# Three low bits of the W1 and W2 words: taken on GpSimd by a product and a minimum, or on VectorE by a shift

## The chip, the core and the metric

One core of one Trainium2 chip runs the whole program. The metric is device time in microseconds (us) of one launch; less is better. The kernel before was timed in three runs, and one further execution was profiled.

## The reference

Three blocks follow each other, for a batch of 8 sequences of 576 rows:

```python
# attention over 32 pooled memory slots per head (8 heads of 64)
a = softmax(phi, axis=2); k_m = einsum('bhsm,bhsd->bhmd', a, k); v_m = einsum(..., a, v)
x = softmax(q @ k_m.T / 8) @ v_m                       # to (B, S, 512)
# first MLP
xn = (x - mean) / sqrt(var + 1e-6) * g_ln
x = x + relu(xn @ w_ch1) @ w_ch2                       # w_ch1 512x2048, w_ch2 2048x512
# second MLP with a spatial gate
h = gelu(x @ w_in); u, v = halves of h
gated = u * (w_sg @ layernorm(v) * g + b_sg)
out = x + gated @ w_out
```

The inputs are float32, except the weights `w_ch1`, `w_ch2` (W1 and W2 below), `w_in` and `w_out`: these are float64, and the kernel gets them as 64-bit words. To make a float32 of such a word the kernel needs the high 32-bit word, shifted and with its exponent moved, and the top three bits of the low 32-bit word.

## The kernel before, in words

The work is split in two phases. Phase 1 does attention and the first MLP, phase 2 the second MLP. In phase 1 a tile is 128 rows; each batch element is cut into two blocks of 256 to 320 columns. For each block `m1` (line 557) multiplies the attention weights with VW, the product of the pooled values and a 512-column quarter of W1; it has no own product x @ W1. ScalarE and VectorE make the ReLU of the result as a high and a low part (`hh` and `hl`, lines 543 and 544), and three steps later (LAG = 3) `m2` multiplies them with a 128-row chunk of W2 (lines 587 to 589). The ring of `hh` and `hl` has four buffers, that of `ph` two.

W1 comes in four quarters of four 128x512 pieces, W2 in sixteen 128x512 chunks: 32 pieces of 512 KB, each loaded once, from SyncE's queue, and converted once. All of this lies between 20 and 145 us of the span. For a piece of W1, `scale_w1` calls `to_f32` and ScalarE scales the result (`wc`, line 476); `center_w1` takes the column mean by TensorE (`cm`, line 482) and subtracts it on VectorE (line 484); `make_vw` multiplies with the pooled values (`pvw`, line 504) and writes `vw` (lines 514 and 515). For a chunk of W2, `split_w2` calls `split`, which makes the high part on ScalarE (line 124) and the low part on GpSimd (line 125). The same `split` with pieces of 256 columns converts `w_in` and `w_out`, in 24 calls around 600 to 850 us.

`to_f32` has three instructions: ScalarE's Prelu on the high word (line 110), VectorE's shift of the low word by 29 (line 111), and VectorE's instruction that shifts the high word and joins the two (line 112). It reads and writes every second 32-bit word of the raw tile, in place.

What sets the order: the program is traced by a list of events with times in steps (`at_time`), W1 quarters loaded at -26.5, -26.2, -2.5 and 2.0 and converted at -16.5, -5.0, 3.0 and 7.5, W2 chunk c loaded 5 units ahead of its conversion. A planner then sorts the instructions of each engine by readiness in a timeline that it works out itself; each engine runs its own list in order. `issue_after(ins)` adds an order edge behind `ins` only for instructions of the engine that `ins` is on. The gates given to `to_f32` are all VectorE instructions (the last `hl`, or, before the first block, an attention instruction on VectorE), so lines 111 and 112 stand behind the gate, and the Prelu on ScalarE does not.

Beside this, the attention of the first batch element runs at 25 to 62 us: scores (line 379), a transpose and a softmax on VectorE (lines 388 to 407) with the exponent on ScalarE (line 393), and the high and low parts of the attention weights, `aTh` and `aTl` (lines 418 and 419; the first `aTl` is on GpSimd). GpSimd's other work in the stretch is the low part of W2 (line 125), sums of exp(phi) (lines 276 to 281), the LayerNorm roots (lines 88 to 98) and `VBl` (line 329).

Of the kernel before, what the change touches and what calls it, by code (L numbers as in the profile page):

```python
# [15 lines left out]
ALU = mybir.AluOpType  # L16
# [12 lines left out]
def fused_kernel(ctx: ExitStack, tc: tile.TileContext, q, k, v, phi, g1, w1, w2, w_in, g2, w_sg, b_sg, w_out, out):  # L29
    nc = tc.nc  # L30
    PE, V, A, G = nc.tensor, nc.vector, nc.scalar, nc.gpsimd
# [11 lines left out]
    TB = 4  # L43
# [32 lines left out]
    wpool = ctx.enter_context(tc.tile_pool(name="wpool", bufs=19))  # L76

    def two(p, dtype, name):
        t = p.tile([P, 2, DM], dtype, tag="w", name=name)
        return t[:, 0, :], t[:, 1, :]  # L80
# [17 lines left out]
            G.tensor_tensor(out=y, in0=y, in1=t, op=ALU.mult)  # L98
        return y

    def to_f32(raw, gate=None):

        words = raw.bitcast(U32).rearrange("p (n two) -> p n two", two=2)
        lo, hi = words[:, :, 0], words[:, :, 1]

        gates = ExitStack()
        for ins in gate or ():
            gates.enter_context(tc.issue_after(ins.ins))
        with gates:
            A.activation(hi.bitcast(F32), hi.bitcast(F32), AF.Prelu, scale=2.0 ** -112, alpha=-(2.0 ** 32))  # L110
            V.tensor_scalar(lo, lo, 29, None, op0=ALU.logical_shift_right)
            V.scalar_tensor_tensor(out=lo, in0=hi, scalar=3, in1=lo, op0=ALU.logical_shift_left, op1=ALU.bitwise_or)
        return lo.bitcast(F32)

    def split(raws, wp, scale=None, gate=None):

        wh, wl = two(wp, F32R, "whl")
        n = DM // len(raws)
        for i, raw in enumerate(raws):
            cs = slice(i * n, (i + 1) * n)  # L120
            h, l = wh[:, cs], wl[:, cs]
            w = to_f32(raw, gate)
            if scale is None:
                A.copy(h, w)
                G.tensor_tensor(out=l, in0=w, in1=h.bitcast(F32), op=ALU.subtract)
            else:
                A.activation(h, w, AF.Copy, scale=scale)
                V.scalar_tensor_tensor(out=l, in0=w, scalar=scale, in1=h.bitcast(F32), op0=ALU.mult, op1=ALU.subtract)
        return wh, wl
# [11 lines left out]
    def phase1():  # L141
# [15 lines left out]
        st = {"lays": [], "ps0": 0}  # L157
# [297 lines left out]
        W2, WC, VW, raws = {}, {}, {}, {}  # L455

        def wc_tiles():
            return [tail.tile([P, 2, DM], F32, tag="wc", name="wc", bufs=4) for _ in range(2)]
# [11 lines left out]
        def scale_w1(fb):  # L470

            WC[fb] = ws = wc_tiles()
            for j, raw in enumerate(raws.pop(fb)):
                d = ws[j // 2][:, j % 2, :]
                w = to_f32(raw, [st.get("hl", tiles[TB - 1]["tr"])] if fb else None)
                A.activation(d, w, AF.Copy, scale=g1c[:, j:j + 1])

        def center_w1(fb):
# [43 lines left out]
        def split_w2(c):  # L522

            gate = st.get("hl", tiles[1 if c == 0 else 3]["tr"])
            W2[c] = split([raws.pop(("w2", c))], wpool, gate=[gate])


        hid, ybank, carry = {}, {}, {}
# [2 lines left out]
        for b in range(B):  # L531
            w = 18 * b
# [62 lines left out]
        tiles = [{"t": t} for t in range(NPAIR * TPP)]  # L595
# [15 lines left out]
        for b in range(B):  # L611
            pair, odd = divmod(b, 2)
            t0 = pair * TPP
            lo, hi = (t0 + 4, 4, 0, 2 * pair), (t0 + 4, 4, REM, 2 * pair + 1)
# [74 lines left out]
        for fb in range(NFB):  # L689
            at_time((-26.5, -26.2, -2.5, 2.0)[fb], load_w1, fb)  # L690
            at_time((-16.5, -5.0, 3.0, 7.5)[fb], scale_w1, fb)
            at_time((-16.4, -0.3, 4.6, 9.1)[fb], center_w1, fb)
            at_time((-15, 1.3, 5.8, 10.3)[fb], make_vw, 0, fb)
            at_time((1.4, 3.0, 7.4, 12.0)[fb], store_w1, fb)
        for c in range(NF):
            split_at = 4.5 * (c // 4) + 0.5625 * (c % 4) - 0.6 if c > 3 else 0.9 * c - 4
            at_time(split_at - 5 if c > 3 else -12.7 if c == 3 else 0.2 * c - 26.4, load_w2, c)
            at_time(split_at, split_w2, c)
# [20 lines left out]
        for n in range(len(steps) + LAG):  # L719
# [4 lines left out]
            if n >= LAG:  # L724
                _, j, c = steps[n - LAG]
# [31 lines left out]
    def convert_piece(p):  # L757
        kind, n = PIECES[p]
        w = split(R.pop(("piece", p)), wpool, 0.5 if kind == 2 else None, None if kind == 2 else R["relu"])
        if kind == 2:  # L760
            WO[n] = w
        else:
            WI[n, kind] = w
# [310 lines left out]
```

## Time and profile before

| what | value |
|---|---|
| median of three runs (lowest, highest) | 1216.44 us (1214.81, 1219.01) |
| the profiled execution's own time | 1217.86 us |
| its span | 1216.1 us |
| granted TensorE clock, mean | 0.987 |
| TensorE matmul busy | 1178.5 us, 97% of the span |
| VectorE / ScalarE / GpSimd busy | 692.4 / 465.8 / 400.6 us |

The span is the time from the first to the last instruction that the profile shows; 1.8 us of the execution's time lie around it. Busy shares are averages over stages that differ: the profile's rows by slices show where TensorE is not full, and the rows by instructions show what ended its waits.

### The profile page before, as it was taken

How to read it: one execution, taken by the hardware profiler on the slowest of the kernel's cores; microseconds unless marked ns; L12 is line 12 of the kernel's file. 1: busy time of each engine (PE TensorE's matmuls, PEld its weight loads, DVE VectorE, ACT ScalarE, POOL GpSimd, SP SyncE). 2: the span in 40 equal slices, each digit the busy share in tenths (PEclk: the TensorE clock that was granted, in tenths of full speed). 3: DMA queues.
4: the chain of work that ended last, by engine and by line, in shares of the span. 5: the costliest groups of instructions: out<-in, count | busy, mean ns of one | idle time of the engine just before them, and what ended most of it. 6: DMA issues, size and time to landing. Idle time of an engine off the chain costs nothing.

```text
span 1216.1 us, 20760 instructions
## 1 busy us (share of the span) xinstructions
PE 1178.5 (97%) x7711; PEld 986.2 (81%) x7711; DVE 692.4 (57%) x1669; ACT 465.8 (38%) x1064; POOL 400.6 (33%) x621
## 2 busy tenths in 40 slices
PE   4599999999999999999999999999999999999998
PEld 2277678878787878888778788889989988998997
DVE  3787665654754545744536546568576367447632
ACT  3575333222332223332223345445444354344430
POOL 2033212211110211211211212456566475656641
PEclk9599999999999999999999999999999999999999
DMA  8996544344413353513332234132250042023202
GB/s 201 270 293 180 164 109 121 95 118 103 105 57 107 82 143 91 131 53 93 84 96 69 81 102 128 35 81 71 78 148 27 19 131 86 1 73 94 78 18 70
DMA packets 199141, 124.15 MB, mean 102 GB/s; under 512 B 93312, under 2 KB 174336, under 8 KB 199040
## 3 DMA queue, kind: packets, MB, share of 16 engines
q1 hardware_dynamic: 199040, 122.82, 36.9%
q8 instruction: 61, 1.00, 0.3%
q14 instruction: 40, 0.33, 0.1%
HBM read 99.72 MB, written 31.33 MB: 108 GB/s over the span
## 4 chain that ended last, share of the span: by engine, by line
PE 88%; DVE 5%; DMA 4%; SPq 1%; issue 1%; ACT 1%; POOL 1%; DVEq 0%; POOLq 0%; ACTq 0%
PE ph L557 16%; PE py L587 11%; PE py L589 11%; PE py L588 10%; PE pvs L976 8%; PE po L999 8%; PE pv L867 8%; PE pu L951 7%; PE pvw L504 2%; PE kvp L299 2%; DMA raw<-in_moe_w_ch_dram 1%; SPq L83 1%; DMA q<-q_d 1%; PE cm L482 1%; PE px L435 1%
## 5 line engine op out<-in xcount | busy, mean ns | idle before, releaser
L557 PE MATMUL ph<-aTh,vw 128*128 128x320 f32 (+1 forms) x1024 | 244.6, 301 | 3.6 <-ACT vw L514 1.7
L587 PE MATMUL py<-whl,hh 128*128 128x512 f32 x512 | 204.5, 401 | 2.8 <-ACT hh L543 2.8
L588 PE MATMUL py<-whl,hh 128*128 128x512 f32 x512 | 202.0, 395 | 0.0
L557 PEld LDWEIGHTS ph<-aTh,vw 128*128 128x128 f32 x1024 | 177.6, 190 | 26.9 <-issue 9.1
L589 PE MATMUL py<-whl,hl 128*128 128x512 f32 x512 | 188.7, 398 | 0.0
L543 ACT ACTIVATE hh<-ph 128x256 fp32r<-128x256 f32 x256 | 97.2, 384 | 155.1 <-PE ph L557 88.0
L544 DVE SCALAR_TENSOR_TENSOR hl<-ph,hh 128x256 fp32r<-128x256 f32 x256 | 106.6, 420 | 83.4 <-ACT hh L543 82.1
L557 PE MATMUL ph<-aTl,vw 128*128 128x256 f32 (+1 forms) x512 | 152.6, 298 | 0.0
L587 PEld LDWEIGHTS py<-whl,hh 128*128 128x128 f32 x512 | 96.3, 188 | 32.9 <-issue 9.8
L976 PE MATMUL pvs<-wsh,vhl 128*128 128x288 f32 x576 | 120.9, 295 | 0.0
L588 PEld LDWEIGHTS py<-whl,hh 128*128 128x128 f32 x512 | 96.6, 189 | 20.8 <-issue 3.4
L951 PE MATMUL pu<-yTh,whl 128*128 128x288 f32 x512 | 110.9, 295 | 0.3 <-DVE ug L856 0.3
L557 PEld LDWEIGHTS ph<-aTl,vw 128*128 128x128 f32 x512 | 97.4, 190 | 10.0 <-issue 2.1
L589 PEld LDWEIGHTS py<-whl,hl 128*128 128x128 f32 x512 | 92.0, 189 | 15.4 <-issue 4.4
L976 PEld LDWEIGHTS pvs<-wsh,vhl 128*128 128x128 f32 x576 | 94.1, 188 | 0.6
L867 PE MATMUL pv<-whl,yTh 128*128 128x512 f32 x288 | 90.8, 395 | 0.0
L999 PE MATMUL po<-whl,gh 128*128 128x512 f32 x288 | 90.1, 391 | 0.0
L951 PEld LDWEIGHTS pu<-yTh,whl 128*128 128x128 f32 x512 | 85.1, 188 | 1.8 <-DVE ug L856 0.8
L543 ACT ACTIVATE cr<-ph 128x64 fp32r<-128x64 f32 x128 | 28.5, 222 | 127.2 <-PE ph L557 126.8
L976 PE MATMUL pvs<-wsl,vhl 128*128 128x288 f32 x256 | 75.4, 295 | 0.0
L951 PE MATMUL pu<-yTl,whl 128*128 128x288 f32 x256 | 75.4, 295 | 0.0
L979 POOL TENSOR_TENSOR gt<-gt,ug 128x288 f32<-128x288 f32 x64 | 52.9, 827 | 68.4 <-DVE gt L978 65.6
(153 smaller groups left out, 2165.4 us busy)
## 6 DMA issues: line engine op xcount, KB each, us to landing
wc<-w_d SPq DMA_DIRECT2D x28, 512.0 KB, 5.0
y_d<-x SPq DMA_DIRECT2D x36, 256.0 KB, 2.8
yt<-y_d SPq DMA_DIRECT2D x36, 256.0 KB, 2.7
yr<-y_d SPq DMA_DIRECT2D x36, 256.0 KB, 3.0
kv<-in_k_dram SPq DMA_DIRECT2D x32, 256.0 KB, 4.0
kv<-in_v_dram SPq DMA_DIRECT2D x32, 256.0 KB, 4.5
raw<-in_moe_w_ch_dram SPq DMA_DIRECT2D x32, 256.0 KB, 8.7
raw<-in_moe_w_ch_dram SPq DMA_DIRECT2D x16, 512.0 KB, 6.2
```

The lines of the kernel that those rows point to most:

```text
L299: mm = PE.matmul(kvp[32 * j:32 * j + 32], ph[:, 4 * g + j, c, :] if c < 4 else pr[rows, j, :], ts[c // 2][0][:, :, j, c % 2, :] if c < 4 e ...
L543: high = A.activation(out_h, src, AF.Relu)
L544: return high, V.scalar_tensor_tensor(out=out_l, in0=src, scalar=0.0, in1=out_h.bitcast(F32), op0=ALU.max, op1=ALU.subtract)
L557: PE.matmul(ph, w_[:, ks], x[:, g, 0:w], start=(n == 0), stop=(n == 3 * HK - 1))
L587: PE.matmul(py, hh, wh, start=start, stop=False)
L588: PE.matmul(py, hh, wl, start=False, stop=False)
L589: PE.matmul(py, hl, wh, start=False, stop=stop)
L867: PE.matmul(pv, y[:, kc, cs], w, start=(n == 0), stop=(n == 3 * KC - 1))
L951: PE.matmul(pu, w[:, ds_], y[:, kc, cs], start=(n == 0), stop=(n == 3 * KC - 1))
L976: PE.matmul(pvs, v_, w_, start=(n == 0), stop=(n == len(ops) - 1))
L979: G.tensor_tensor(out=gt, in0=gt, in1=ug, op=ALU.mult)
L999: PE.matmul(po, gg[:, dc, cs], w, start=(n == 0), stop=(n == 3 * KC - 1))
```

## The change

In the calls for W1 and W2 the low word goes to GpSimd, which multiplies it by 2^-29 and takes the minimum with 7, in one instruction that reads and writes 32-bit integers. The calls for `w_in` and `w_out` pass no engine and keep the shift on VectorE. The joining instruction of line 112 stays on VectorE.

```diff
-    def to_f32(raw, gate=None):
+    def to_f32(raw, gate=None, low=None):
...
-            V.tensor_scalar(lo, lo, 29, None, op0=ALU.logical_shift_right)
+            if low is None:
+                V.tensor_scalar(lo, lo, 29, None, op0=ALU.logical_shift_right)
+            else:
+                low.tensor_scalar(lo, lo, 2.0 ** -29, 7.0, op0=ALU.mult, op1=ALU.min)
...
-    def split(raws, wp, scale=None, gate=None):
+    def split(raws, wp, scale=None, gate=None, low=None):
...
-            w = to_f32(raw, gate)
+            w = to_f32(raw, gate, low)
...
-                w = to_f32(raw, [st.get("hl", tiles[TB - 1]["tr"])] if fb else None)
+                w = to_f32(raw, [st.get("hl", tiles[TB - 1]["tr"])] if fb else None, G)
...
-            W2[c] = split([raws.pop(("w2", c))], wpool, gate=[gate])
+            W2[c] = split([raws.pop(("w2", c))], wpool, gate=[gate], low=G)
```

## Rows read from the trace of the kernel before

**Rows 1.** The page: TensorE's busy tenths in 40 slices of the span.
```profile
PE   4599999999999999999999999999999999999998
```
**Rows 2.** Busy time by stretches: us, engines' busy us (instructions), clock, DMA share, GB/s.
```profile
25.00:45.00 20.00, 8.05 (x51) 3.28 (x49) 11.41 (x26) 10.03 (x17) 0.85 (x2) 0.72 1.04 249
45.00:57.00 12.00, 8.06 (x32) 4.19 (x32) 10.83 (x25) 5.93 (x12) 2.58 (x2) 0.50 1.04 262
57.00:65.00 8.00, 7.17 (x27) 5.01 (x28) 6.88 (x15) 5.52 (x11) 1.30 (x1) 0.73 1.03 385
65.00:145.00 80.00, 78.32 (x521) 59.53 (x519) 60.81 (x137) 44.92 (x101) 28.92 (x35) 1.00 0.74 207
```
**Rows 3.** Groups by shape, VectorE, the shift: busy us, mean ns, idle before.
```profile
L111 DVE TENSOR_SCALAR raw<-raw 128x512 uint32<-128x512 uint32 x32 | 14.6, 488 | 7.7 <-DMA raw<-in_moe_w_ch_dram 7.7
```
**Rows 4.** The same view for GpSimd: the nearest forms.
```profile
L125 POOL TENSOR_TENSOR whl<-raw,whl 128x512 fp32r<-128x512 f32 x16 | 20.8, 1314 | 54.1 <-ACT whl L124 49.1 <-issue 3.0 <-DMA raw<-in_moe_w_ch_dram 1.9
L402 POOL TENSOR_TENSOR z<-z,r 128x512 f32<-128x512 f32 x14 | 14.7, 1049 | 134.2 <-DVE r L401 59.0 <-ACT hh L543 28.6 <-ACT cr L543 14.2
L155 POOL MEMSET VBh<- 128x512 f32 x2 | 1.0, 524 | 0.0
```
**Rows 5.** ScalarE in order of time: start us, us, work, idle before.
```profile
33.45 0.67 ACT L110 ACTIVATE raw<-raw 128x512 f32<-128x512 f32 x1 [0.92 <-DMA raw<-in_moe_w_ch_dram]
...
40.32 0.67 ACT L110 ACTIVATE raw<-raw 128x512 f32<-128x512 f32 x1 [1.58 <-DMA raw<-in_moe_w_ch_dram]
40.89 0.61 ACT L393 ACTIVATE z<-z 128x512 f32<-128x512 f32 x1
42.56 0.66 ACT L110 ACTIVATE raw<-raw 128x512 f32<-128x512 f32 x1 [1.06 <-DMA raw<-in_moe_w_ch_dram]
...
49.96 0.66 ACT L110 ACTIVATE raw<-raw 128x512 f32<-128x512 f32 x1 [2.03 <-DMA raw<-in_moe_w_ch_dram]
```
**Rows 6.** VectorE in order of time.
```profile
37.67 0.69 DVE L391 TENSOR_REDUCE m<-z 128x16 f32<-128x512 f32 x1
41.53 0.69 DVE L399 TENSOR_REDUCE r<-z 128x16 f32<-128x512 f32 x1 [3.18 <-ACT z L393]
...
45.30 0.41 DVE L111 TENSOR_SCALAR raw<-raw 128x512 uint32<-128x512 uint32 x1
45.63 0.17 DVE L400 TENSOR_SCALAR r<-r 128x16 f32<-128x16 f32 x1
45.71 2.34 DVE L484 TENSOR_TENSOR wc<-wc,cm 128x1024 f32<-128x1024 f32 x2
...
53.74 2.44 DVE L111 TENSOR_SCALAR raw<-raw 128x512 uint32<-128x512 uint32 x7
```
**Rows 7.** TensorE in order of time.
```profile
36.02 6.04 PE L482 MATMUL cm<-wc,mean 128*128 128x512 f32 x8
46.98 3.06 PE L504 MATMUL pvw<-wc,kvT 64*32 64x512 f32 x16 [4.91 <-DVE wc L484]
...
57.83 2.08 PE L482 MATMUL cm<-wc,mean 128*128 128x512 f32 x2 [0.88 <-ACT wc L476]
```
**Rows 8.** TensorE's waits in the stretch of 105 to 115 us.
```profile
PE ph L557 <- DVE hl L544: 0.8, 1, 0.8
```
**Rows 9.** VectorE in order of time, late in phase 1's conversions.
```profile
110.02 1.55 DVE L111 TENSOR_SCALAR raw<-raw 128x512 uint32<-128x512 uint32 x1
...
141.20 1.27 DVE L400 TENSOR_SCALAR r<-r 128x4 f32<-128x4 f32 x1
```
**Rows 10.** GpSimd in order of time.
```profile
47.19 1.28 POOL L419 TENSOR_TENSOR aTl<-z,aTh 128x512 fp32r<-128x512 f32 x1 [21.27 <-ACT aTh L418]
...
109.98 1.30 POOL L125 TENSOR_TENSOR whl<-raw,whl 128x512 fp32r<-128x512 f32 x1
...
139.84 2.60 POOL L125 TENSOR_TENSOR whl<-raw,whl 128x512 fp32r<-128x512 f32 x2 [3.04 <-issue]
```
**Rows 11.** Durations of the joining instruction by tile: min, median, max ns.
```profile
L112 DVE SCALAR_TENSOR_TENSOR raw<-raw x32: 674/686/1236, 26.5 to 139.0; 128x512 uint32<-128x512 uint32 x32
```

## The prediction

> **What bounds the kernel now.** I read the slices of the page first: TensorE is at nine tenths or more from the third slice on, and only the first two (to 61 us) show 4 and 5 [rows 1]. So for 95% of the span any other engine's relief is worth nothing unless it ends a TensorE wait. The 32 conversions that the change touches all lie in 25 to 145 us, so I next took busy time by stretches there [rows 2]. In 25 to 45 us TensorE works 8.05 of 20 us, in 45 to 57 it works 8.06 of 12 at a granted clock of 0.50 (the 1.2 GHz level) with VectorE busy 10.83 of 12, and in 57 to 65 it works 7.17 of 8. In 65 to 145 it works 78.32 of 80. The time that VectorE could give back sits before 58 us, with 1.7 us of TensorE idle behind it.
>
> The views in order of time then say which wait ends last there. The weights land one piece per 2.2 us (starts at 40.32 and 42.56 that end a wait for a load [rows 5]), with the transfer engines fully busy [rows 2]. VectorE waits until 41.53 for the exponent of the softmax, and that exponent stood on ScalarE behind a Prelu that waited for a load until 40.32 [rows 5, 6]. From 41.53 to 45.71 VectorE works without a gap up to the centering of the first W1 quarter (line 484), for which TensorE sits idle 4.91 us until 46.98 [rows 6, 7]. The column means themselves were done at 36.02 + 6.04 = 42.06 [rows 7], so VectorE's chain is late there by 45.71 - 42.06 = 3.65 us. The second place is at 57.83: TensorE waits 0.88 us for `wc` of the second quarter, and in front of that on VectorE stand seven shifts of 2.44 us in all, and right behind them line 112 [rows 6, 7].
>
> **The change part by part.** Profiled execution: 1217.86 us, of which the span is 1216.1.
>
> *The removed shifts.* 32 x 488 ns, which is the 14.6 us of the row [rows 3], leave VectorE. On the path are: (a) the one at 45.30, which holds up line 400 until 45.63: -0.33 us, all of it in front of the idle TensorE [rows 6]. (b) The seven at 53.74: line 112 can start some 2.4 us earlier, but TensorE gets only the 0.88 us that it waited, since it is in its own work right up to that wait [rows 7]: -0.9. What is late next there is TensorE itself at the lower clock. (c) The other 24 shifts are between the four of the first quarter, which run beside a longer Prelu (0.67 us, as at 33.45 [rows 5]) and so cost nothing now, and those beside a full TensorE; one wait of TensorE there is for VectorE's `hl`, 0.8 us [rows 8], behind the shift of 1.55 us at 110.02 [rows 9]: -0.8. Below: the same three and nothing more. Above: none of (b) and (c), if another instruction takes the place, -0.3.
>
> *The added instruction.* No row shows a wide GpSimd instruction with one input and integers. From below stands the memset of 128x512, 524 ns, which reads nothing; from above the two-input subtraction of line 125, 1314 ns [rows 4]. I take the product of line 402, 1.05 us: it is the nearest, a product whose second input is one value per 32 elements. 32 x 1.05 = 34 us (17 to 42) are added to a GpSimd that is busy 0.85 + 2.58 + 1.30 + 28.92 = 33.7 of these 120 us [rows 2]; the sum is 56% of it, so the engine holds it. Nothing of VectorE's gate holds the new instruction: like the Prelu it goes as soon as its load has landed, well ahead of line 112 in most cases (a Prelu at 49.96 at the latest for the pieces whose shifts stand at 53.74 [rows 5, 6]). In the first quarter it is 1.05 - 0.67 = 0.4 us later than the Prelu, so line 112, `wc` and the column mean slip 0.4 us (-0.15 to +0.65); that lies under the 3.65 us above and costs nothing. If that cover went, it would cost the 0.4.
>
> *What queues behind it.* The new instruction waits for a load at the head of GpSimd's list. Behind it before 57 us stands the first `aTl`, at 47.19 [rows 10]; ScalarE's own waits for the same loads were 1 to 2 us [rows 5], and the first matmuls start only after TensorE's 16 of 3.06 us from 46.98 [rows 7], so `aTl` has room for one such wait. Cost 0, at most 1. SyncE's list changes only where a raw buffer comes free, at line 125 or `wc`, which move by less than a microsecond; 0.
>
> *Held instructions on VectorE.* A short VectorE instruction that meets a running GpSimd one is stretched: line 400 took 1.27 us at 141.20 where its like takes 0.17 [rows 6, 9], and it ended at 142.47, GpSimd's pair at 142.44 [rows 10]; the shift at 110.02 ended at 111.57, GpSimd's subtraction at 111.28. In 41.5 to 45.7 us GpSimd is idle today. With the change an instruction starts there for each landing, at 42.56 and about 44.9, and VectorE has two-input and short scalar instructions there for roughly half the time. Two meetings of up to 1.05 us give 0 to +2.1; I take +0.8. Later, where TensorE is full, line 112 itself was held once in its 32 (1236 ns against a median of 686 [rows 11]); with twice the GpSimd time this may touch one wait: 0 to +0.8, I take +0.3.
>
> *Sum.* -0.3 - 0.9 - 0.8 + 0.8 + 0.3 = -0.9 us: 1217.86 - 0.9 = 1217.0 for the profiled execution. This execution lies 1.4 us over the median of the three runs, and the forecast is for such a median: 1216.44 - 0.9 = 1215.5. The ends are -2.0 and +3.6 (all holds, `aTl` late, only (a) kept). A measurement of this kernel tells some 0.3%, 3.65 us, from no change, so this is "the same". Own range of this case: 1214.4 to 1220.0, from these ends on the median.
>
> **The rivals.**
>
> *Faster, by the order on ScalarE.* With fewer VectorE instructions and later joins the planner may sort the first exponent ahead of the Prelu that waits for a load. VectorE had done its maximum at 38.36 and then idled 3.18 us for it [rows 6]. Then line 484 is bound by the column means at 42.06 in place of 45.71: -3.65, and with -0.9 and -0.8 it is -5.3: 1211. For it: all of this stands on the path and TensorE waits 4.91 us there [rows 7]. Against: neither the Prelu nor the exponent is in the diff, and their readiness changes little.
>
> *Slower, by holds in the chain from 41.5 to 57 us.* If a GpSimd instruction is long, or one runs at nearly every moment there, the VectorE instructions before line 484 and before line 112 are held one after the other. From 42.56 on a piece lands every 2.2 us [rows 5], which makes seven before 57. At a hold of 1.27 - 0.17 = 1.1 us [rows 6, 9] four holds (4.4) outweigh what leaves (2.0) and from six on, 6.6 - 2.0 = +4.6, it is measurable: 1221. For it: lines 400, 402 and 392 come again and again there. Against: one held instruction lets the others run behind the end of the same GpSimd instruction.
> The Trainium skill, "SBUF — State Buffer", section "Who interferes with whom", says that VectorE and GpSimd share one pair of ports under an exclusive lock, and that a VectorE instruction with two SBUF inputs, or a fast-mode tensor_scalar, waits for the whole GpSimd instruction if that came first. By that rule the two meetings above would be full ones, +2.1 in place of +0.8, and the forecast 1216.8; the ends that coincide at 142.47 and 142.44 agree with it [rows 9, 10].
>
> *Slower, since the integer form is slow on GpSimd.* A price t above 1314 ns is not excluded by any row. Against 2.2 us per landing GpSimd falls behind from t = 2.2 on; the four pieces of the first quarter, the fourth landed at 33.45 [rows 5] and the first some 3 x 2.24 us before, at 26.7, then end at 26.7 + 4t in place of 34.1, and the 3.65 us of cover are used up at t = 2.8. At t = 4 the centering is 26.7 + 16 - 34.1 - 3.65 = 5 us later, and the pieces of the second quarter stand in the same line, so +6 and 1222 at least.
>
> *It relieves nothing.* The shifts' time is filled by other waits, and the time stays at 1216.4. This has the forecast's sign of "the same" and is held with it.
>
> **Chances.** Forecast, with the case that nothing moves: 0.58. Faster by the order: 0.22. Holds: 0.12. Slow form: 0.08. So faster by over 0.3% 0.22, within 0.3% 0.58, slower 0.20. The range takes the faster rival's 1211 and the holds' 1221, and leaves out the slow form and the tails beyond.
>
> **What would show it.** Right: 32 GpSimd instructions on raw tiles near 1.05 us, starts at the landings; TensorE's idle before the first `pvw` 4.6 to 5.8 us and that before `cm` at 57 gone; VectorE's busy time lower by some 12 us. Holds show as line 400, 402 or 112 at over 1 us with an end at a GpSimd end. Wrong: a first `pvw` before 45 or after 49 us, a GpSimd instruction of over 2.2 us, or a new TensorE wait after 65 us behind a join or an `aTl`.

## The result and the profile after

The changed kernel takes 1233.9 us (median of six runs, 1231.4 to 1237.7) against 1216.4 us before: a ratio of 1.0146, with a 95% interval of 1.013 to 1.0163. The forecast was no change, 1215.5 us; the range of the case was 1214.4 to 1220.0, and with the rivals taken in 1211 to 1221. It is slower, by 17.5 us.

The profiled execution of the changed kernel took 1231.38 us with a span of 1229.3, 13.2 us more than before. Line numbers move by three behind `to_f32`: line 125 is now 128, 278 is 281, 419 is 422, 482 is 485, 543 is 546, 557 is 560; the joining line 112 is 115, and the new GpSimd instruction is line 114. The page, parts 1 and 2 (busy us and share; TensorE's busy tenths and granted clock in 40 slices):

```profile
PE 1182.3 (96%) x7711; PEld 986.9 (80%) x7711; DVE 683.6 (56%) x1637; ACT 465.1 (38%) x1064; POOL 466.9 (38%) x653
...
PE   4598889999999999999999999999999999999998
...
PEclk9599989999999999999999999999999999999999
```

Three of the slices, the fourth to the sixth (92 to 184 us), now stand at 8, where [rows 1] has 9 throughout. The same stretches as in [rows 2], after the change (us, then busy us and instructions of TensorE, its weight loads, VectorE, ScalarE, GpSimd; clock, DMA share, GB/s):

```profile
25.00:45.00 20.00, 9.10 (x48) 2.88 (x48) 9.41 (x21) 9.76 (x17) 18.31 (x10) 0.60 1.03 254
45.00:57.00 12.00, 6.42 (x22) 1.92 (x22) 11.39 (x19) 7.57 (x14) 11.52 (x7) 0.50 1.05 264
57.00:65.00 8.00, 7.44 (x31) 4.61 (x31) 6.08 (x13) 5.11 (x12) 6.13 (x5) 0.83 1.00 364
65.00:145.00 80.00, 70.92 (x447) 54.42 (x446) 44.74 (x92) 37.30 (x81) 58.90 (x45) 0.98 0.59 170
```

Two columns tell it. GpSimd, 0.85 and 2.58 us busy in the first two stretches of [rows 2], is now busy 18.31 of 20 and 11.52 of 12. And in 65 to 145 us, where TensorE had worked 78.32 of 80, it works 70.92: 7.4 of the 13.2 us are idle time of TensorE in the stretch that was full. VectorE is busy 16 us less there, and nothing is gained by it.

GpSimd by shape in 25 to 145 us (busy us, mean ns, idle before):

```profile
L114 POOL TENSOR_SCALAR raw<-raw 128x512 uint32<-128x512 uint32 x32 | 67.4, 2106 | 5.3 <-DMA raw<-in_moe_w_ch_dram 2.9
L128 POOL TENSOR_TENSOR whl<-raw,whl 128x512 fp32r<-128x512 f32 x14 | 18.4, 1319 | 7.8 <-ACT whl L127 5.6 <-DMA raw<-in_moe_w_ch_dram 1.6
```

VectorE's join in the same view of 20 to 160 us:

```profile
L115 DVE SCALAR_TENSOR_TENSOR raw<-raw 128x512 uint32<-128x512 uint32 x32 | 26.6, 854 | 10.3 <-POOL raw L114 10.3
```

The new instruction takes 2106 ns, twice the 1.05 us that the sum used and well over the 1314 ns of the upper bound [rows 4]. GpSimd in order of time (start us, us, count):

```profile
26.76 25.16 POOL L114 TENSOR_SCALAR raw<-raw 128x512 uint32<-128x512 uint32 x11 [1.06 <-DMA raw<-in_moe_w_ch_dram]
52.00 1.31 POOL L422 TENSOR_TENSOR aTl<-z,aTh 128x512 fp32r<-128x512 f32 x1
...
69.52 10.46 POOL L114 TENSOR_SCALAR raw<-raw 128x512 uint32<-128x512 uint32 x5
80.06 0.73 POOL L88 TENSOR_TENSOR rs_t<-ve,mhalf 128x2 f32<-128x2 f32 x1
80.87 8.30 POOL L114 TENSOR_SCALAR raw<-raw 128x512 uint32<-128x512 uint32 x4
...
91.78 0.19 POOL L95 TENSOR_TENSOR rs_t<-rs_t 128x2 f32<-128x2 f32 x1
...
104.90 0.74 POOL L279 TENSOR_TENSOR sm<-phi 128x256 f32<-128x256 f32 x1
...
119.36 0.73 POOL L281 TENSOR_TENSOR sm<-sm,phi 128x256 f32<-128x256 f32 x1
...
128.58 1.31 POOL L128 TENSOR_TENSOR whl<-raw,whl 128x512 fp32r<-128x512 f32 x1 [4.68 <-ACT whl L127]
129.84 1.19 POOL L281 TENSOR_TENSOR sm<-sm,phi 128x256 f32<-128x256 f32 x1
...
132.67 0.98 POOL L284 TENSOR_TENSOR sm<-sm,phir 64x128 f32<-64x128 f32 x2
```

Read it from the short instructions: the first LayerNorm root has its first step at 80.06 and its second at 91.78, and the sum of exp(phi) of the second batch element, five additions, runs from 104.90 to 133.65. The first `aTl`, at 47.19 in [rows 10], starts at 52.00. In the kernel before, the same sum stood so, and ended at 111.24 + 1.57 = 112.81:

```profile
106.85 0.88 POOL L276 TENSOR_TENSOR sm<-phi 128x256 f32<-128x256 f32 x1 [1.21 <-ACT phi L270]
...
111.24 1.57 POOL L281 TENSOR_TENSOR sm<-sm,phir 64x128 f32<-64x128 f32 x2
```

The sum does not start late: its first addition is at 104.90, 2 us ahead of the kernel before. It is stretched, from 6.0 to 28.8 us. Between its first and its last addition the list of the kernel before has one low part; that of the changed kernel has four new instructions (8.0 us), six low parts (7.8 us) and five steps of the LayerNorm roots (1.4 us), and GpSimd idles 8.1 us between them. The largest gap is the 4.68 us in front of 128.58: the low part of a W2 chunk (line 128) waits there for ScalarE, and three of the five additions stand behind it in the list. What TensorE makes of it, first by its records of `ptsum`, the transpose of that sum (min, median, max ns, first and last start):

```profile
L287 PE MATMUL ptsum<-ident,sm x2: 328/328/329, 133.2 to 135.0; 128*128 128x128 f32 x2
```

And in order of time:

```profile
115.11 0.38 PE L560 MATMUL ph<-aTh,vw 128*128 128x256 f32 x1 [2.64 <-DVE hl L547]
...
135.82 3.70 PE L485 MATMUL cm<-wc,mean 128*128 128x512 f32 x8 [0.17 <-DVE rs L289]
140.47 1.08 PE L302 MATMUL kvp<-kv,phi 128*32 128x128 f32 x32 [0.95 <-DMA kv<-in_v_dram]
...
142.61 1.09 PE L507 MATMUL pvw<-wc,kvT 64*32 64x512 f32 x16 [0.70 <-DVE pvw L502]
144.41 0.39 PE L560 MATMUL ph<-aTh,vw 128*128 128x256 f32 x1 [0.71 <-ACT vw L517]
```

The same `ptsum` in the kernel before:

```profile
L284 PE MATMUL ptsum<-ident,sm x2: 270/300/329, 114.3 to 115.3; 128*128 128x128 f32 x2
```

It is 19 us later. From 133 to 144.41 us TensorE has only the second batch element's preparation and the column means of the last W1 quarter (`cm`) in its list, step behind step (`ptsum`, `kvp`, `cm`, `pvw`, `vw`), with nothing of the big products between; it works 8.74 of these 11.41 us. How late each product of the first layer starts against the kernel before, counted from the two traces (the n-th group of six matmuls of line 557 or 560):

```
n          0     2     6    12    16    20    22    24    30    48    240
before  51.7  61.0  73.2  92.1 102.6 112.0 118.4 133.2 147.0 213.7  748.5
after   52.0  64.4  74.9  90.1 106.9 117.3 124.4 144.4 160.8 225.8  761.8
later    0.3   3.4   1.7  -2.0   4.3   5.3   6.0  11.2  13.8  12.1   13.3
```

From 170 us on the difference only swings between 10 and 16 us, and from 280 on it stands at 13.4. It arises in four places: from the 12th to the 16th product (90 to 107 us) it goes from 2.0 ahead to 4.3 behind, 1 to 2 us come by the 22nd, 5 between the 22nd and the 24th, at the late sum, and the last 2 to 3 by the 30th (160 us). TensorE's lists interleave the products differently in the two kernels, so single ones swing by some us (the 23rd is 1.7 us late).

### The profile page after: what moved, and what is told of

The parts are those of the page before. It is cut to its first block, busy times and chain, and to the rows that moved or that the text cites. A ratio compares the mean times of both kernels' runs of the same rounds, so it can differ in the third digit from the quotient of the medians.

```text
span 1229.3 us, 20782 instructions
## 1 busy us (share of the span) xinstructions
PE 1182.3 (96%) x7711; PEld 986.9 (80%) x7711; DVE 683.6 (56%) x1637; ACT 465.1 (38%) x1064; POOL 466.9 (38%) x653
## 4 chain that ended last, share of the span: by engine, by line
PE 86%; DMA 4%; DVE 4%; SPq 2%; issue 1%; ACT 1%; POOL 1%; POOLq 0%; DVEq 0%; ACTq 0%
PE ph L560 16%; PE py L590 10%; PE py L592 10%; PE py L591 10%; PE pvs L979 8%; PE po L1002 8%; PE pv L870 8%; PE pu L954 7%; PE pvw L507 3%; DMA raw<-in_moe_w_ch_dram 3%; SPq L83 2%; PE kvp L302 2%; DMA q<-q_d 1%; PE cm L485 1%; PE px L438 1%
```

## The experiments

Theories: **price** (the instruction is dearer than assumed, GpSimd is full, and its older work queues behind it: also called the queue), **join** (the join now waits for another engine), **order** (the planner's lists change when the shift leaves VectorE) and **holds** (VectorE is stretched whenever GpSimd runs).

**Half the width (e1_half).** Line numbers differ by a few from kernel to kernel below.

```diff
-                low.tensor_scalar(lo, lo, 2.0 ** -29, 7.0, op0=ALU.mult, op1=ALU.min)
+                low.tensor_scalar(lo[:, 0:256], lo[:, 0:256], 2.0 ** -29, 7.0, op0=ALU.mult, op1=ALU.min)
...
-            V.scalar_tensor_tensor(out=lo, in0=hi, scalar=3, in1=lo, ...)
+            V.scalar_tensor_tensor(out=lo, in0=hi, scalar=3, in1=nil.to_broadcast([P, DM]), ...)
```

> GpSimd takes 256 of the 512 low words of each piece; the joining instruction takes a zero in their place, so the three low bits are left out and the rest of the work is as in the changed kernel. Theory PRICE (the instruction takes 2.1 us in place of 1.05, GpSimd is full from 27 to 125 us, and its older work queues behind it): the instruction is 1.0 to 1.15 us, which is the price that the prediction assumed, GpSimd is busy about 70 of 120 us, and the time is 1215 to 1220. Rival JOIN (VectorE's join now waits for another engine, whatever its price): 1224 or more. Rival ORDER (the planner's lists change because the shift left VectorE): 1228 or more. Rival HOLDS (every busy us of GpSimd holds VectorE): half the loss, 1223 to 1226.

Measured: 1217.2 us against 1217.6 before on the same chip, ratio 0.9996 (0.9983 to 1.0008). The instruction took 1169 ns in the mean:

```profile
L116 POOL TENSOR_SCALAR raw<-raw 128x256 uint32<-128x256 uint32 x32 | 37.4, 1169 | 12.3 <-DMA raw<-in_moe_w_ch_dram 10.5
```

At the price that the prediction assumed, its result comes true. Join, order and holds each had said 1223 or more. Join falls with this run: the joins wait 11.4 us for GpSimd, and the time is level.

```profile
L118 DVE SCALAR_TENSOR_TENSOR raw<-raw,nil 128x512 uint32<-128x512 uint32 x32 | 23.8, 773 | 11.4 <-POOL raw L116 11.4
```

The price is not all that differs, though. The planner's list for GpSimd is another one too: one new instruction stands between the first and the second addition of the sum, where the changed kernel has three, and the sum ends at 114.10 us.

**Two columns (e2_none).** The same with `lo[:, 0:2]`.

> GpSimd takes 2 of the 512 low words, the join takes a zero: the price is near 0.25 us, the dependence of the join on GpSimd stays, the shifts are gone from VectorE, the low bits are left out. PRICE: 1213 to 1217, at or a little under the kernel before. JOIN: 1220 to 1226. ORDER: 1228 or more. HOLDS: 1214 to 1217.

Measured: 1210.3 us, ratio 0.9946 (0.9923 to 0.997): faster than all theories had it. The instruction takes 275 ns. Order falls in the form in which it was put: the shift has left VectorE in both runs, and neither is slower. That a list changes with the price, as above, these runs do not test. The join depends on GpSimd here too, but GpSimd is done before ScalarE's Prelu, which is what the joins wait for (12.1 us). Part of the 7 us shows in the stretches, in the columns of above:

```profile
45.00:57.00 12.00, 9.42 (x44) 4.58 (x45) 10.94 (x21) 8.04 (x16) 3.38 (x5) 0.86 1.02 287
57.00:65.00 8.00, 8.00 (x54) 5.72 (x53) 5.15 (x13) 6.19 (x14) 5.36 (x11) 1.00 1.04 357
```

And in TensorE's order of time:

```profile
45.97 3.07 PE L510 MATMUL pvw<-wc,kvT 64*32 64x512 f32 x16 [4.87 <-DVE wc L490]
50.20 0.39 PE L563 MATMUL ph<-aTh,vw 128*128 128x256 f32 x1 [1.17 <-ACT vw L520]
50.43 0.28 PE L563 MATMUL ph<-aTl,vw 128*128 128x256 f32 x1
```

The granted clock is 0.86 in 45 to 57 us in place of 0.50 [rows 2], and the first product of the first layer already runs at the 2.4 GHz level: 0.28 us per matmul of 256 columns, as only from 61 us on in the kernel before, where the same matmul took 0.41 at 52 us. The work of 50 to 61 us thus takes less time. Counted as in the table above, the products of this run lead those of the kernel before by 1.5 us at the first, 3.3 at the 2nd, 5.6 at the 12th, 5.5 at the 30th and 9.0 at the 48th: the clock's stretch holds less than half of it. The last 3.5 come at 150 us, where TensorE in the kernel before waits 1.75 us for ScalarE's `hh` and here does not. This is one profiled execution; why the clock rose at 50 us here and at 55 in the run at half width was not tried.

**The load without the dependence (e3_dead).** The kernel before, plus, behind the join:

```diff
+            if raw.shape[1] == DM:
+                G.tensor_scalar(hi, hi, 2.0 ** -29, 7.0, op0=ALU.mult, op1=ALU.min)
```

> The kernel before with its shifts on VectorE, and beside them the same GpSimd instruction (product and minimum, 128x512, in place) 32 times on the high words after the join, where nobody reads them any more. GpSimd's load is that of the changed kernel, but no join waits for it. PRICE: GpSimd's sums and LayerNorm roots queue behind it all the same, so most of the loss is there, 1224 to 1236. JOIN: 1215 to 1218. ORDER: 1215 to 1219. HOLDS: 1226 to 1234, with joins and line 400 stretched to over 1 us.

Measured: 1238.4 us, ratio 1.017 (1.0146 to 1.0194). No join waits for these instructions, and the loss is there in full and more, past the upper end of what price had said. GpSimd is busy 90.7 of the 120 us from 25 to 145, and the transposes of the sum are later still:

```profile
L286 PE MATMUL ptsum<-ident,sm x2: 475/476/476, 141.8 to 144.0; 128*128 128x128 f32 x2
```

This run doesn't part price from holds, which had 1226 to 1234. By the code it also keeps each raw buffer until GpSimd is done with it, W1's too, which the changed kernel does not; what that costs was not tried.

**The price by itself (e4_forms).** The kernel before with one more instruction per W2 piece on its dead raw tile, in eight forms.

```diff
+            if f == 0: G.tensor_scalar(s, s, 2.0 ** -29, 7.0, op0=ALU.mult, op1=ALU.min)
+            elif f == 1: G.tensor_scalar(s, s, 2.0 ** -29, None, op0=ALU.mult)
...
+            else: G.tensor_copy(out=s, in_=s)
```

> The kernel before with one GpSimd instruction more for each of the 16 pieces of W2, on the raw tile when it is dead, in eight forms, two of each: to measure the disputed price by itself. If the integer conversion is the price, the float32 form of product and minimum takes 1.0 to 1.3 us and the integer one 2.0; if the step over every second word is, the form on adjacent words is near 1.0; if the second operation is, the product alone is near 1.0 to 1.2; if all forms take 2.0 us, a one-input GpSimd instruction of 512 elements costs more than a two-input one (1.31 us).

Durations by line (min, median, max ns of two): product and minimum on every second word as integers (527) and as float32 (531), on adjacent words as integers (535) and as float32 (537); the product alone on every second word, integers (529) and float32 (533); the copy (541). The lowest of the two is the undisturbed one.

```profile
L527 POOL TENSOR_SCALAR raw<-raw x2: 2011/2186/2362, 49.5 to 104.3; 128x512 uint32<-128x512 uint32 x2
...
L529 POOL TENSOR_SCALAR raw<-raw x2: 1597/2091/2585, 60.9 to 109.1; 128x512 uint32<-128x512 uint32 x2
L531 POOL TENSOR_SCALAR raw<-raw x2: 2000/2156/2313, 63.6 to 113.1; 128x512 f32<-128x512 f32 x2
L533 POOL TENSOR_SCALAR raw<-raw x2: 1572/1572/1573, 67.0 to 117.6; 128x512 f32<-128x512 f32 x2
L535 POOL TENSOR_SCALAR raw<-raw x2: 1923/1924/1924, 84.0 to 125.7; 128x512 uint32<-128x512 uint32 x2
L537 POOL TENSOR_SCALAR raw<-raw x2: 1917/2116/2316, 86.8 to 129.1; 128x512 f32<-128x512 f32 x2
...
L541 POOL COPY raw<-raw x2: 637/646/654, 91.3 to 147.8; 128x512 uint32<-128x512 uint32 x2
```

Neither the integers (2011 against 2000 ns) nor the step (2000 against 1917) is the price: it is the instruction with numbers as operands. The second operation costs 0.4 us, the first 0.9 over a copy. The program took 1228.5 us in one run, 16 such instructions more.

**The sum moved (e5_sums_v).** The changed kernel, and in `prep_sum`:

```diff
+            E = V if b == 1 else G
-            G.tensor_tensor(out=sm, in0=ph[:, :, 0, :], in1=ph[:, :, 1, :], op=ALU.add)
+            E.tensor_tensor(out=sm, in0=ph[:, :, 0, :], in1=ph[:, :, 1, :], op=ALU.add)
...
```

> The changed kernel, with the five additions that sum exp(phi) of the second batch element (lines 279 to 284 there) on VectorE in place of GpSimd; nothing else. In the changed kernel the last of them ends at 133.6 us, where it ended at 112.8 before, and the first ptsum of TensorE moves from 114.3 to 133.2. QUEUE (GpSimd's older work stands behind the new instruction, and TensorE runs dry behind this sum): ptsum at 112 to 120 us, the step of about 5 us between the 22nd and the 24th product of the first layer goes, and the time is 1225 to 1230. Rival PIECES (what is late is the conversion of the pieces itself, the sum is only seen there): ptsum is early, and the time stays at 1232 to 1236.

Measured: 1222.2 us against 1217.9, ratio 1.0033 (1.0019 to 1.0047): five additions on another engine give back some 13 of the 17.5 us, each kernel against the one before on its own chip (17.5 and 4.3 us slower), more than was expected. `ptsum` comes before it did in the kernel before:

```profile
L288 PE MATMUL ptsum<-ident,sm x2: 272/302/331, 107.9 to 108.8; 128*128 128x128 f32 x2
```

The 24th product is 2.0 us late in place of 11.2; the 22nd is still 10.8 late, since TensorE did the second element's preparation ahead of it. GpSimd is as full as before (98.8 of 120 us), so a busy GpSimd alone, by holds, doesn't cost these 13 us. The rival (pieces) falls.

**Its control (e9_before_sums_v).** The same edit on the kernel before.

> The kernel before, with the five additions of the second batch element's sum on VectorE in place of GpSimd: the control of the run with the sums moved. QUEUE: in the kernel before GpSimd was idle around this sum, so the move gives little, 1213 to 1219, and the 11 us that it gave in the changed kernel are its queue. Rival: the move is a gain of its own whatever GpSimd does, some 10 us, 1205 to 1210.

Measured: 1217.4 against 1216.5 us, ratio 1.0008 (0.9994 to 1.0021): the move is worth nothing where the additions follow each other and GpSimd is not full.

**W1 alone, W2 alone (e6_w1_only, e7_w2_only).** `G` is passed in one of the two calls only.

```diff
-            W2[c] = split([raws.pop(("w2", c))], wpool, gate=[gate], low=G)
+            W2[c] = split([raws.pop(("w2", c))], wpool, gate=[gate])
```

> The changed kernel with GpSimd for the 16 pieces of W1 alone; the pieces of W2 are shifted on VectorE as before. QUEUE, with GpSimd's load between 25 and 145 us at 34 + 16 x 2.1 = 67 us, which is the load of the half-width run: 1214 to 1221. If each new instruction costs the same wherever it stands: half the loss, 1224 to 1227.

> The changed kernel with GpSimd for the 16 pieces of W2 alone. QUEUE, the same load of 67 us: 1214 to 1221. If each new instruction costs the same wherever it stands: 1224 to 1227. With the run of W1 alone: if the two losses add up to much less than 16 us, the loss comes with the saturation and not piece by piece.

Measured: W1 alone 1217.2 us, ratio 0.9995 (0.9983 to 1.0007); W2 alone 1224.2 us, ratio 1.0049 (1.0033 to 1.0065), at the low edge of the rival's range and outside the queue's. The loads are alike (66.0 and 65.0 of 120 us), so the load alone doesn't decide: the W1 pieces come between 25 and 89 us, ahead of the sum, those of W2 in part beside it. The first `ptsum` is at 115.2 us with W1 and at 126.9 with W2. The two add up to some 6 us, against 17.5 for both together.

W2 alone also bears on the run with two columns. Its clock in 45 to 57 us is 0.86 too, and its first products run at the 2.4 GHz level; then TensorE waits 3.86 us and goes on at the 1.2 GHz level (two `cm` in 2.07 us, as at 57.83 in [rows 7]).

```profile
45.00:57.00 12.00, 6.21 (x32) 2.62 (x32) 11.32 (x23) 6.04 (x12) 9.81 (x6) 0.86 1.04 255
...
51.28 0.28 PE L560 MATMUL ph<-aTl,vw 128*128 128x256 f32 x1
...
58.42 2.07 PE L485 MATMUL cm<-wc,mean 128*128 128x512 f32 x2 [3.86 <-ACT wc L479]
```

An early rise of the clock is thus not a gain by itself.

**The product alone (e8_product).** One operation, with a factor that never rounds up to 8.

```diff
-                low.tensor_scalar(lo, lo, 2.0 ** -29, 7.0, op0=ALU.mult, op1=ALU.min)
+                low.tensor_scalar(lo, lo, 0.9374 * 2.0 ** -29, None, op0=ALU.mult)
```

> The changed kernel with the product alone, by 0.9374 x 2^-29, so that no word rounds to 8 and the minimum is not needed; all else is as changed. The product alone took 1.57 us in the run of the forms, so GpSimd's load is 34 + 32 x 1.6 = 85 of 120 us. From the three prices measured (0.28 us: -7, 1.17: 0, 2.1: +16) PRICE gives 1221 to 1227. If the number of operations in an instruction did not matter beyond its own time, the low parts and sums would still queue: same range; at 1232 or more the price is not what decides.

Measured: 1226.6 us, ratio 1.0063 (1.0045 to 1.0082), inside the range; `ptsum` at 124.3. With price the time goes: 0.28 us: -7, 1.17: 0, 1.64: +9, 2.1: +17.5; the lists go with it.

**ScalarE, and a mix (e10_scalar, e11_mixed).** First all 32 pieces by ScalarE, then W1 on GpSimd as in the change and W2 on ScalarE.

```diff
-                low.tensor_scalar(lo, lo, 2.0 ** -29, 7.0, op0=ALU.mult, op1=ALU.min)
+                A.activation(lo, lo, AF.Copy, scale=0.9374 * 2.0 ** -29)
```

> The changed kernel with the low words on ScalarE: a copy with scale 0.9374 x 2^-29, integers in and out, in place of GpSimd's product and minimum; nothing left out. ScalarE's Prelu on the same words takes 0.67 us, so 32 x 0.67 = 21 us on a ScalarE that is busy 66 of 120 us. QUEUE: GpSimd is free again and VectorE is relieved of its shifts as in the run with two columns, which gained 7 us; ScalarE's chain of Prelus and exponents grows by some 3 us at the start: 1209 to 1216. Rival: ScalarE becomes what the ReLU waits for: 1219 or more.

> W1's 16 pieces on GpSimd by product and minimum, W2's 16 on ScalarE by the scaled copy; VectorE has no shift of either; nothing left out. GpSimd's load is 67 of 120 us as in the run of W1 alone, which was level with the kernel before; ScalarE's grows by 16 x 0.67 = 11 us. QUEUE: 1210 to 1217. Rival: the queue on GpSimd is already long at 67 us once VectorE no longer is what TensorE waits for: 1218 or more.

Measured: ScalarE 1218.0 us, ratio 1.0006 (0.9992 to 1.0021), between the two expectations: 655 ns each, and no gain. The mix 1214.8 us against 1216.5, ratio 0.9982 (0.9971 to 0.9992): a little faster than the kernel before, some 2 us, and 19 us faster than the changed one.

## Why the prediction was wrong, point by point

*What bounds the kernel* held for where the difference arises, before 170 us. But the stretch from 65 to 145 us was read as full and so as safe: full says that little can be gained there, and the loss arose there.

*The added instruction* is the first step that failed: "1.05 us", bounded by 524 and 1314 ns. It measured 2106 ns. The bound from above was no bound: a two-input subtraction on GpSimd says nothing about an instruction with two numbers and two operations. The trace had no wide one; its rows of 128x1 and 128x2 show only some 0.2 us and say nothing of the width. At half the width, with 1.17 us, the time is level: the loss comes with the price above that, and with the list that goes with the price. The Trainium skill, "GPSIMD Engine Reference", section "Engine selection", calls one-input work on GpSimd roughly line-rate. The copy of 512 words took 0.65 us, as ScalarE's scaled copy of as many did (0.655), which agrees; the runs disagree for the product (1.57 us) and for product and minimum (1.9 to 2.1).

*"The sum is 56% of it, so the engine holds it"* failed with it: 33.7 + 67.4 = 101 of 120 us (94.9 of it inside the stretch, the rest slid behind), and as the pieces are ready early most of it stands at the front. From 26.8 to 110 us GpSimd hardly stops (78.3 of 83.2 us).

*What queues behind it* is the step that carries the loss: "cost 0, at most 1". Only the first `aTl` was looked at. The sum of exp(phi), much further down the list, was not: the kernel before had it ready at 112.8 and the changed one at 133.65, 21 us later, and moving it alone gives back some 13 us. The order of GpSimd's list is the planner's, and it puts pieces of W1 and W2 between the five additions: the sum is late by what stands between its additions, of which the new instructions are 8.0 us, and not by a late start. How the loss is shared between that order and the engine's full list was not tried apart.

*SyncE's list*, put at 0 in the same step, was wrong too: raw buffers were to come free within a microsecond of before. The last two loads of pieces are issued from 110.64 us on, where the kernel before had 101.20:

```profile
101.20 2.74 SPq L83 DMA_DIRECT2D raw<-in_moe_w_ch_dram  x2
...
110.64 2.16 SPq L83 DMA_DIRECT2D raw<-in_moe_w_ch_dram  x2
```

The first row is of the kernel before, the second of the changed one. The runs with the sum moved and with the mix issue theirs from 114.11 and 108.98 us on and are 4.3 us slower and not slower at all, so late loads are not what the 13 us are.

*The removed shifts*, -2.0 us, may have been priced too low. The run with two columns gains 7.3 us (0.3 to 0.8% with its interval, 3.6 to 9.4 us), more than that term. But how much of it the shifts are is not shown: the run with the low words on ScalarE has no shift of W1 and W2 on VectorE either and gains nothing, 3.5 us of the lead arise at 150 us, at a wait that the term did not name, and the clock that rises before the first products, which it did not foresee, rose so early in the slower run of W2 alone as well. That this gain is what balances the price at half the width is likewise not shown.

*Held instructions* were rightly seen in the kernel before (though the joining instruction was held twice there, 1236 and 1223 ns, and not once), but what they would cost was not: +0.8 us in the chain from 41.5 us on. Line 400, now 403, took 0.17 us there beside the new instructions, which run one behind the other from 26.76 to 51.92. The join's mean went from 726 to 854 ns, 32 x 0.13 = 4 us of VectorE's time, on an engine that had 16 us less to do in 65 to 145. Three VectorE rows, then the GpSimd rows beside the second and the third:

```profile
42.26 0.17 DVE L403 TENSOR_SCALAR r<-r 128x16 f32<-128x16 f32 x1
...
108.34 1.32 DVE L115 SCALAR_TENSOR_TENSOR raw<-raw 128x512 uint32<-128x512 uint32 x1
...
114.97 0.68 DVE L115 SCALAR_TENSOR_TENSOR raw<-raw 128x512 uint32<-128x512 uint32 x1
...
107.81 1.30 POOL L128 TENSOR_TENSOR whl<-raw,whl 128x512 fp32r<-128x512 f32 x1
...
113.66 2.00 POOL L114 TENSOR_SCALAR raw<-raw 128x512 uint32<-128x512 uint32 x1 [1.84 <-DMA raw<-in_moe_w_ch_dram]
```

The Trainium skill, "SBUF — State Buffer", section "Who interferes with whom", has a two-input VectorE instruction wait for the whole GpSimd one. The trace agrees for the two-input subtraction of line 128: the join at 108.34 ends 0.56 us behind it, and so, by 0.54 to 0.55 us, do the ones at 100.40 (1800 ns, the longest), 129.16 and 150.29. It disagrees for the new one-input instruction: the join at 114.97, in the midst of one that runs until 115.66, took 0.68 us, where the median is 690 ns, and the five longest that met only the new instruction, all begun in its first 0.6 us, took 1.07 to 1.14.

*The rivals.* Slower by the form's price was the right direction, with 8 in 100, but its place was wrong: it wanted 2.2 us per landing and a late first quarter, and the first `pvw` came at 47.89, only 0.9 us late. The point from which the price decides lies lower, between 1.17 and 1.6 us, since GpSimd's own work has to fit too.

*Open:* the quarter of the loss that stays when the sum is moved; the lateness that arises at 90 to 107 us; and the wait of 2.64 us at 115.11, where ScalarE stood before a late load (its row: 3.24 us idle for a W piece at 113.67). No run took them alone.

## What to carry to other kernels

Before moving work to an idle engine, list that engine's own instructions of the same stretch with the engine that waits for each: here five additions of 4 us in all, well off the path, became the path. An engine's share over the whole span (33%) says nothing of a stretch in which the new work is ready at once and its list is worked in order; add the loads stretch by stretch, and where the sum nears the stretch, price the last consumer. Look at the list's order as well: here work was late behind other instructions that waited, on an engine that idled. A price without a row of the same operation, the same count of operands and the same width has no upper bound; measure it on dead data first.

## What the runs showed of the hardware

GpSimd's instruction with numbers as operands costs 1.57 to 1.60 us with one operation and 1.92 to 2.01 us with two on 128x512 when undisturbed, nearly alike for integers and float32 and, with two operations, for adjacent and every second word, where a copy takes 0.65 us and a two-tensor subtraction 1.31. Joins on VectorE that met that subtraction ended 0.54 to 0.56 us behind it; beside the new one-input instruction they took 0.68 to 0.77 us, and five that began in its first 0.6 us 1.07 to 1.14. ScalarE does the same conversion of integers, scaled, in 0.655 us. TensorE's granted clock was 0.86 in 45 to 57 us in the run with two columns and 0.50 both before and after the change, with 9.42 us of its work there in place of 8.06 and 6.42; it was 0.86 with 6.21 us of work in the run of W2 alone.
